# Decode attention on one Trainium2 core: the output weights loaded in eight parts that shrink, instead of three

## The chip, the cores and the metric

The kernel runs on one core of one Trainium2 chip (trn2). The metric is device time in microseconds (us) of one execution; smaller is better. Every run that is quoted was in the fast (undisturbed) state, and profiles are compared with profiles of that state. The profiled span, from the core's first to its last instruction, is some 1.9 us shorter than the device time.

## The reference, cut to what matters

One decode step for two sequences: attention with grouped heads over a long cache, an output projection, a gate from a small MLP, and a residual.

```python
B, Sq, D = 2, 1, 512
Hq, Hkv, Sk, Dh = 32, 8, 32768, 128          # all tensors bf16
...
q = (xn @ wq) ...
scores = einsum("bhqd,bhkd->bhqk", q, k) * Dh ** -0.5
o = einsum("bhqk,bhkd->bhqd", softmax(scores), v)
s = o.reshape(B, Sq, Hq * Dh) @ wo           # wo: 4096 x 512, 4 MB
return x + s * silu(mlp(xn))
```

K and V are 268 MB together. Each is read once, so the kernel is a long stream of loads with arithmetic running beside it. `wo` (4 MB) is the last thing that is loaded.

## The kernel before

The 16 pairs of sequence and K/V head are worked off one after the other. All large loads are issued from SyncE (SP) on one DMA queue, two large buffers being refilled in turn. The projection weights `wo` go into the part of `kbuf` that the last group no longer needs; they are issued behind the last V load, in three parts of four, three and one K/V heads:

```python
    wo_parts = [(0, 4), (4, 7), (7, 8)]
    ...
    for m in range(NG):                       # NG = 16 groups
        ...                                   # scores of one K half, next K load, the other half
        for i in range(NPART):
            emit_v(m, hs[i], i, eps[i])       # P times V; the last half also normalises into oX
        if not last:
            load_v(*groups[m + 1], 2 if m == NG - 2 else 1)
        if m == NG - 2:
            wo3 = kbuf[:, 0:Hq * D].rearrange("p (g c) -> p g c", g=Hkv)
            wos = A_wo.rearrange("(g p r) d -> p g (r d)", p=128, r=NQ)
            for a, z in wo_parts:
                nc.sync.dma_start(out=wo3[:, a:z, :], in_=wos[:, a:z, :])
```

The tail is 128 small matmuls, 16 for each K/V head, that accumulate into `s_ps`. Then come two VectorE steps (`sg`, the gate, and `out4`, the residual) and two stores of 1 KB each, one from SyncE and one from ScalarE:

```python
    for gr in range(Hkv * NQ):
        g, r = divmod(gr, NQ)
        for n in range(NQ):
            c = r * D + n * QW
            nc.tensor.matmul(s_ps[32 * n:32 * n + B, :], lhsT=oX[:, g, r, :],
                             rhs=wo3[:, g, c:c + QW], ...)
    ...
    for b, eng in ((0, nc.sync), (1, nc.scalar)):
        eng.dma_start(out=out[b, 0, :].rearrange("(n c) -> n c", c=QW), in_=out4[b:QP:32, :])
```

The framework gives every load and store that is issued from SyncE or ScalarE one of eight completion semaphores, in turn.

The softmax here doesn't subtract the row's maximum and nothing guards it: scores larger than these inputs give would overflow.

## Time and profile before

| | before |
|---|---|
| time, median of 3 runs | 660.86 us (660.72 to 660.88) |
| profiled span | 658.9 us |
| bytes moved, rate over the span | 280.9 MB, 426 GB/s |
| last packet of `wo` written | 653.68 us |
| `sg` starts | 654.71 us |
| SyncE issues its output store | 655.43 us |

The page of the kernel before comes first. Its DMA row gives the busy share of the 16 DMA engines in tenths for each of 40 slices; the queue rows give packets, megabytes and share of the engines' time; the last line gives shares of the chain that ended last.

```profile
span 658.9 us, 6323 instructions
...
DMA  9999999999999999999999999999999999999995
...
q1 hardware_dynamic: 6408, 280.50, 98.6%
q8 instruction: 21, 0.34, 0.2%
...
q14 instruction: 7, 0.06, 0.0%
...
DMA 75%; DVE 14%; issue 7%; PE 3%; SPq 0%; ACT 0%; DVEq 0%
```

The loads bound the kernel from start to end. What a change to `wo` can reach is the last slice. The timeline of that slice, before (start in us, duration, engine, line, operation, count; in brackets the engine's idle time before it and what ended it):

```profile
649.70 1.09 PE L400 MATMUL s_ps<-kbuf,oX 128*2 128x128 bf16 x64
652.79 1.88 PE L400 MATMUL s_ps<-kbuf,oX 128*2 128x128 bf16 x64 [2.00 <-DMA kbuf<-in_A_wo_dram]
654.71 0.29 DVE L408 TENSOR_TENSOR sg<-s_ps,g 98x128 f32<-98x128 f32 x1 [4.53 <-PE s_ps L400]
655.11 0.29 DVE L410 TENSOR_TENSOR out<-sg,x 98x128 bf16<-98x128 f32 x1
655.43 0.66 SPq L412 DMA_DIRECT2D out_dram<-out  x1
655.43 0.61 ACTq L412 DMA_DIRECT2D out_dram<-out  x1
```

PE does the first four heads at once, waits 2.00 us for the second part, and then has 64 matmuls to do in one piece.

The third view is busy time by stretch of the tail, before (stretch, its length, busy us and instructions of five engines, granted clock, DMA share, GB/s):

```profile
647.50:649.50 2.00, 1.08 (x12) 0.99 (x9) 0.16 (x1) 0.59 (x1) 0.00 (x0) 1.00 0.97 387
649.50:652.50 3.00, 1.26 (x68) 1.07 (x68) 0.34 (x2) 0.00 (x0) 0.00 (x0) 0.68 0.54 220
652.50:654.00 1.50, 1.21 (x48) 1.21 (x48) 0.00 (x0) 0.00 (x0) 0.00 (x0) 0.50 0.26 101
```

The DMA engines do not stop together. From 649.5 us on about half of them still work, and from 652.5 on five of 16 (the share of 0.26 takes in the last 0.3 us, when these too have ended). The landing records of the last part show it: seven engines report by 650.00 us, four by 652.44 and five by 653.99. Only the slowest ones decide when a part of `wo` has landed.

### The profile page before, as it was taken

What the parts mean: (1) busy time and instruction counts of PE and PEld (TensorE: products, weight loads), DVE (VectorE), ACT (ScalarE), POOL (GpSimd) and SP (SyncE); (2) the same over time, 40 slices, a digit from 0 to 9 for tenths busy, and PEclk for the clock granted to TensorE, in tenths of its full rate; (3) what the DMA queues carried; (4) which work ended last, traced back from release to release, by engine and by line L of the source; (5) the groups of instructions that cost most, each with busy time, mean ns of one, the idle gap of its engine ahead of it and who ended that gap; (6) DMA issues with size and microseconds to landing.
All of it is one profiled execution on the core that took longest, in us unless ns stands there. A gap on an engine that the chain in (4) does not pass through costs nothing.

```text
span 658.9 us, 6323 instructions
## 1 busy us (share of the span) xinstructions
PE 386.7 (59%) x2652; PEld 172.1 (26%) x2684; DVE 346.0 (53%) x442; ACT 50.3 (8%) x152; POOL 6.9 (1%) x20
## 2 busy tenths in 40 slices
PE   2338194673828557283764729377482946738764
PEld 2313132231313223131331313123131322313322
DVE  5147192754809265381935629183572918447560
ACT  1301001010100101000010100101010010100000
POOL 4000000000000000000000000000000000000000
PEclk9999688786968968697886959878596877859896
DMA  9999999999999999999999999999999999999995
GB/s 367 451 426 442 435 446 439 410 443 426 439 438 435 430 435 422 447 434 423 442 427 442 438 419 434 443 434 443 414 423 446 443 442 443 410 427 428 431 421 224
DMA packets 6704, 280.91 MB, mean 426 GB/s; under 512 B 906, under 2 KB 916, under 8 KB 1940
## 3 DMA queue, kind: packets, MB, share of 16 engines
q1 hardware_dynamic: 6408, 280.50, 98.6%
q8 instruction: 21, 0.34, 0.2%
q0 software_dynamic: 256, 0.01, 0.0%
q14 instruction: 7, 0.06, 0.0%
q10 hardware_dynamic: 12, 0.00, 0.0%
HBM read 280.50 MB, written 0.00 MB: 426 GB/s over the span
## 4 chain that ended last, share of the span: by engine, by line
DMA 75%; DVE 14%; issue 7%; PE 3%; SPq 0%; ACT 0%; DVEq 0%
DMA kbuf<-in_A_k_cache_dram 69%; DVE T L303 14%; DMA kbuf<-in_A_wo_dram 6%; PE sc L311 2%; PE o L343 1%; PE s_ps L400 0%; ACT ep L320 0%; SPq L95 0%; DVE pt L322 0%; SPq L115 0%; SPq L392 0%; SPq L114 0%; SPq L101 0%; PE S L339 0%; DVE sg L408 0%
## 5 line engine op out<-in xcount | busy, mean ns | idle before, releaser
L311 PE MATMUL sc<-T,z 128*128 128x512 bf16 x992 | 276.4, 421 | 206.3 <-DVE T L303 197.8
L303 DVE STREAM_TRANSPOSE T<-kbuf 128x1024 int32<-128x1024 int32 x256 | 291.5, 1205 | 150.5 <-DMA kbuf<-in_A_k_cache_dram 150.5
L311 PEld LDWEIGHTS <-z 128*128 128x128 bf16 x1024 | 105.7, 103 | 371.2 <-issue 278.7
L343 PE MATMUL o<-vbuf,pt 128*16 128x512 bf16 x1024 | 69.9, 434 | 3.2 <-DMA vbuf<-in_A_v_cache_dram 3.2
L320 ACT ACTIVATE ep<-sc 128x512 bf16<-128x512 f32 x32 | 19.1, 597 | 493.2 <-PE sc L311 451.2
L334 DVE MEMSET o<- 128x512 f32 x16 | 7.8, 485 | 69.3 <-ACT ob L352 68.3
L322 DVE STREAM_TRANSPOSE pt<-ep 128x512 bf16<-128x512 bf16 x32 | 22.6, 707 | 34.7 <-ACT ep L320 34.4
L343 PEld LDWEIGHTS <-pt 128*16 128x16 bf16 x1024 | 27.2, 99 | 37.9 <-issue 18.2
L339 PE MATMUL S<-sm,ones_f 128*128 128x4 f32 x64 | 10.7, 238 | 26.1 <-DVE sm L338 26.1
L355 PE MATMUL oT<-sel_o,ob 128*128 128x4 f32 x128 | 16.9, 255 | 11.1 <-ACT ob L352 11.1
L355 PEld LDWEIGHTS oT<-sel_o,ob 128*128 128x128 f32 x128 | 15.5, 191 | 19.3 <-ACT ob L352 19.3
L339 PEld LDWEIGHTS S<-sm,ones_f 128*128 128x128 f32 x64 | 10.7, 188 | 30.9 <-DVE sm L338 28.4
L352 ACT COPY ob<-o 128x512 f32<-128x512 f32 x16 | 9.4, 586 | 83.4 <-PE o L343 83.4
L362 DVE TENSOR_TENSOR on<-oT,rec 128x4 bf16<-128x4 f32 x16 | 2.6, 162 | 21.8 <-PE oT L355 21.8
L286 ACT COPY z<-qr 32x16 bf16<-32x16 bf16 x64 | 12.6, 198 | 11.5 <-DVE qr L233 10.9
L360 DVE RECIPROCAL rec<-S 128x4 f32<-128x4 f32 x16 | 2.9, 182 | 7.6 <-PE S L339 7.6
L365 PEld LDWEIGHTS <-sel_r 128*128 128x128 bf16 x64 | 5.2, 117 | 5.2 <-issue 5.2
L320 ACT ACTIVATION_READ_ACCUMULATOR ep<-sc 128x1 f32 x32 | 6.3, 198 | 0.2
L215 PE MATMUL qT_ps<-xT,kbuf 128*128 128x2 bf16 x128 | 3.6, 165 | 4.5 <-DMA kbuf<-in_A_wq_dram 4.5
L365 PE MATMUL xp<-on,sel_r 128*128 128x4 bf16 x64 | 3.8, 164 | 4.1 <-DVE on L362 4.1
L338 DVE TENSOR_SCALAR sm<-sel_h,rs 128x4 f32<-128x4 f32 x32 | 6.0, 188 | 0.0
L370 DVE TENSOR_TENSOR xm<-xp,mask 128x16 f32<-128x16 f32 x16 | 2.8, 174 | 5.3 <-PE xp L365 5.3
(64 smaller groups left out, 48.5 us busy)
## 6 DMA issues: line engine op xcount, KB each, us to landing
kbuf<-in_A_k_cache_dram SPq DMA_DIRECT2D x2, 4096.0 KB, 29.1
vbuf<-in_A_v_cache_dram SPq DMA_DIRECT2D x2, 4096.0 KB, 26.7
kbuf<-in_A_wq_dram SPq DMA_DIRECT2D x1, 4096.0 KB
vbuf<-in_B_w_dram SPq DMA_DIRECT2D x2, 1792.0 KB, 21.6
kbuf<-in_A_wo_dram SPq DMA_DIRECT2D x1, 2048.0 KB, 35.9
kbuf<-in_A_wo_dram SPq DMA_DIRECT2D x1, 1536.0 KB, 39.1
kbuf<-in_A_wo_dram SPq DMA_DIRECT2D x1, 512.0 KB
kbuf<-in_A_k_cache_dram SPq DMA_DIRECT2D x15, 29.4
```

Of the source, the lines that this page charges most:

```text
L286: nc.scalar.copy(out=z[32 * j:32 * j + 32, :, :, c:c + rep], in_=qr[32 * j:32 * j + 32, :, :, b, g * rep:(g + 1) * rep],)
L303: nc.vector.transpose(out=T[:, :].rearrange("p (b t k) -> p t b k", b=NB, t=RT), in_=kt[:, r * W:(r + 1) * W].rearrange("p (t b k) -> p t ...
L311: nc.tensor.matmul(sc[:, :], lhsT=z[:, nb, e, zc:zc + 128], rhs=Tb[:, nb, :, e], start=(r == 0 and nb == 0 and e == 0), stop=(r == NR - 1 ...
L320: nc.scalar.activation(out=ep[:, :], in_=sc[:, :], func=ACT.Exp, scale=inv_sqrt_dh, accum_out=rs[:, :])
L322: nc.vector.transpose(out=pt[:, :, :].rearrange("p r (t h) -> p t r h", h=rep), in_=ep[:, :].rearrange("p (t r h) -> p t r h", r=NR, h=rep),)
L334: nc.vector.memset(state["o"][:, :], 0.0)
L338: nc.vector.tensor_scalar_mul(out=sm[:, :], in0=sel_h[:, :], scalar1=rs[:, 0:1])
L339: nc.tensor.matmul(S[:, :], lhsT=ones_f[:, :], rhs=sm[:, :], start=(i == 0), stop=(i == NPART - 1))
L343: nc.tensor.matmul(o[32 * j:32 * j + VT * rep, :], lhsT=pt[:, r, a * VT * rep:(a + 1) * VT * rep], rhs=vt[:, u * VT:(u + 1) * VT, :].rearr ...
L352: nc.scalar.copy(out=ob[:, :], in_=o[:, :])
L355: nc.tensor.matmul(oT[:, :], lhsT=ob[:, t * Dh:(t + 1) * Dh], rhs=sel_o[:, t, :], start=(t == 0), stop=(t == VT - 1),)
L365: nc.tensor.matmul(xp[:, r, :], lhsT=sel_r[:, r, :, :].rearrange("p j w -> p (j w)"), rhs=on[:, :], start=True, stop=True,)
```

## The change

The intent is that PE should work off `wo` as it arrives, and that almost nothing should be left to do when the last bytes land. The last head is cut into 256, 128 and 128 KB.

```diff
-    wo_parts = [(0, 4), (4, 7), (7, 8)]
+    wo_parts = [
+        (0, 2, 0, 4), (2, 4, 0, 4), (4, 5, 0, 4), (5, 6, 0, 4),
+        (6, 7, 0, 4), (7, 8, 0, 2), (7, 8, 2, 3), (7, 8, 3, 4),
+    ]
...
-            for a, z in wo_parts:
-                nc.sync.dma_start(out=wo3[:, a:z, :], in_=wos[:, a:z, :])
+            for a, z, c, e in wo_parts:
+                nc.sync.dma_start(
+                    out=wo3[:, a:z, c * D:e * D], in_=wos[:, a:z, c * D:e * D]
+                )
```

## The prediction

> **What bounds the kernel now.** The load stream. The page gives 280.9 MB in 658.9 us, 426 GB/s, the DMA row of the 40 slices is almost all 9; the chain of waits is 75% DMA. So only the tail after the last byte can move. The timeline there: the second half of the last V releases PE at 644.15 us; the last attention group runs to 650.2; 64 projection matmuls (heads 0 to 3) start at 649.70; PE then idles 2.00 us for wo; at 652.79 the second part (three heads) lands and 64 matmuls run without a break for 1.88 us (29 ns each, granted clock 0.5); `sg` starts at 654.71, the output is issued at 655.43, the span ends at 658.9.
>
> The DMA packets in the trace add what the timeline hides. The 16 DMA engines are not in step: completions of one transfer come from seven engines first, five some 2.8 us later, four some 4.3 us later. In half-microsecond windows the DMA share falls from 1.0 to 0.6 at 649.5 and to 0.3 at 652.5. Every landing is that of the slowest four. They end the second wo part near 652.43, 0.36 us before PE starts on it, and the third near 653.68, which so reaches PE near 654.04. PE comes to that head (after 48 matmuls) near 654.2. Between that landing and `sg` lie about 0.65 us, all that finer parts can shorten.
>
> **What the change does.** Same 4 MB, order and queue.
> - Removes: the backlog. Heads 4, 5 and 6 land 1.25 us apart, near 650.3, 651.5 and 652.8, worked off as they come; after the last 128 KB four matmuls remain instead of a run of 64. PE tail after the last landing from 0.65 to about 0.2 us: -0.45 us.
> - Adds: shorter packets. A packet of 32 KB took 1,213 ns, one of 4 KB 159 ns, which gives about 8 ns per packet beside the bytes (estimate). Half of the last head then goes in 2 KB and half in 1 KB pieces: per engine 8 x 84 + 16 x 46 = 1.40 us against 1.27, +0.13 us. Five more completions: no cost shows in the spacing of the parts (1.248 us), so 0 to 0.1. The Trainium skill, "DMA: Bandwidth & Descriptors", section Bandwidth, gives 0.95 us for a 64 KB transfer and says to batch to 1 MiB or more, which should not apply to parts queued behind others.
> - Moves: in the built order 32 projection matmuls stand before the last group's last steps (21 before `oT`, 11 before `xp`). They need the first 1 MB, which should land near 646.7, before `o` ends at 647.5, and fit into PE's 0.7 us wait for the ScalarE copy. The last two wo transfers wait for the V halves' semaphores (eight are shared), at the latest near 644.7, with some 3 us of queue still ahead. No cost.
>
> **Sum.** -0.45 + 0.13 + about 0.05 = -0.3 us of 660.86, or 0.04%. Predicted 660.6 us, 659.9 to 661.2. Chances: faster by over 2% 0.005, within 2% 0.99, slower by over 2% 0.005.
>
> **What would show it.** `sg` starts 0.2 to 0.5 us earlier; the DMA still ends near 653.8; PE has several short waits for wo instead of one of 2.00 us; just four matmuls after the last; span 0.1 to 0.5 us shorter.
>
> **What would make it wrong.** 1 KB packets costing 100 ns or more; the late issue starving engines (DMA share falling before 649); the reordered matmuls delaying `oT` past 648.3; a different skew of the DMA engines.

## The result, and the profile after

| | before | after |
|---|---|---|
| time, median of 4 runs each | 660.79 us (660.57 to 660.88) | 659.69 us (659.62 to 659.87) |
| ratio of fast runs, 95% interval | | 0.9984 (0.9969 to 0.9998) |
| profiled span | 658.9 us | 658.0 us |

A ratio is the mean time of one kernel's fast runs over the mean of the other's fast runs of the same rounds, so it is not quite the ratio of the medians quoted here. The gain is 1.10 us where 0.3 had been forecast, and 659.69 lies below the predicted range.

The timeline of the tail, after (columns as before):

```profile
646.54 0.50 PE L405 MATMUL s_ps<-kbuf,oX 128*2 128x128 bf16 x21 [0.56 <-DMA kbuf<-in_A_wo_dram]
...
649.00 0.81 PE L405 MATMUL s_ps<-kbuf,oX 128*2 128x128 bf16 x32 [0.49 <-DMA kbuf<-in_A_wo_dram]
...
650.32 0.60 PE L405 MATMUL s_ps<-kbuf,oX 128*2 128x128 bf16 x16 [0.51 <-DMA kbuf<-in_A_wo_dram]
...
651.54 0.59 PE L405 MATMUL s_ps<-kbuf,oX 128*2 128x128 bf16 x16 [0.63 <-DMA kbuf<-in_A_wo_dram]
...
654.07 0.09 PEld L405 LDWEIGHTS <-oX 128*2 128x2 bf16 x3 [0.23 <-issue]
654.39 0.29 DVE L413 TENSOR_TENSOR sg<-s_ps,g 98x128 f32<-98x128 f32 x1 [5.46 <-PE s_ps L405]
...
655.11 0.65 SPq L417 DMA_DIRECT2D out_dram<-out  x1
```

Busy time by stretch, after (columns as before):

```profile
649.50:652.50 3.00, 1.50 (x44) 0.91 (x36) 0.00 (x0) 0.00 (x0) 0.00 (x0) 0.50 0.56 223
652.50:654.00 1.50, 1.20 (x28) 0.67 (x28) 0.00 (x0) 0.00 (x0) 0.00 (x0) 0.50 0.27 94
```

Up to `sg` everything is as forecast. The single wait of 2.00 us has become several short ones. Only the last four matmuls run after the last landing (the line at 654.07 has the weights of three of them; those of the first were loaded ahead). `sg` starts at 654.39 instead of 654.71, 0.32 us earlier. The stream ends at the same place: the last packet of `wo` is written at 653.74 instead of 653.68. The two halves of the DMA tail look the same.

The rest of the gain lies behind `sg`. From `sg` to the end of the span the kernel before took 658.94 - 654.71 = 4.22 us and the changed one 658.00 - 654.39 = 3.61 us, a difference of 0.61 us, although both execute the same two VectorE steps and the same two stores there. The trace has SyncE's closing list of waits. These are the starts of its entries in us, with the landings of the two stores between them (listed from the trace's records; S is a semaphore):

```
before   656.15 S110   656.23 S100   [landed: 657.10 S102, 657.27 S113]
         657.11 S102   657.29 S113   657.76 S114   657.85 S115   657.92 S116   657.99 S117   658.05 S118
after    655.82 S110   655.89 S100   655.96 S102   656.02 S113   656.08 S114   656.14 S115   656.20 S116
         [landed: 656.75 S118, 657.04 S117]   657.06 S117   657.12 S118
```

Each entry takes about 62 ns. Before, the stores had the semaphores that stand third and fourth in the list of nine entries (102, 113), so SyncE stopped there until the output had landed and still had five entries to go through. One of those steps, from 657.29 to 657.76, took 0.47 us instead of 0.06. After, five more transfers had moved the turn of the eight semaphores on by five. The stores now have the last two (117, 118), and the other entries are passed while the output is still in flight.

From the last landing to the end of the span: 658.94 - 657.27 = 1.66 us before, 658.00 - 657.04 = 0.96 us after. The flight of the stores (SyncE's issue to the last landing) was 1.84 us before and 1.94 us after. So the 0.93 us between the spans are 0.32 (up to `sg`), -0.09 (flight) and 0.70 (closing list). The remaining 0.17 us between the spans' difference and that of the medians is within the spread of the runs: the profiled run of the changed kernel was its slowest (659.87 us, 0.18 above the median).

### The profile page after: what moved, and what is told of

It reads as the page before. It is cut to its first block, busy times and chain, and to the rows that moved or that the text cites. A ratio compares the mean times of both kernels' runs of the same rounds, so it can differ in the third digit from the quotient of the medians.

```text
span 658.0 us, 6362 instructions
## 1 busy us (share of the span) xinstructions
PE 393.5 (60%) x2684; PEld 172.1 (26%) x2684; DVE 345.4 (52%) x442; ACT 50.2 (8%) x152; POOL 6.9 (1%) x20
## 4 chain that ended last, share of the span: by engine, by line
DMA 75%; DVE 15%; issue 7%; PE 2%; ACT 0%; SPq 0%; DVEq 0%
DMA kbuf<-in_A_k_cache_dram 69%; DVE T L303 14%; DMA kbuf<-in_A_wo_dram 5%; PE sc L311 1%; PE o L343 1%; PE s_ps L405 0%; PE oT L355 0%; DVE pt L322 0%; ACT ep L320 0%; ACT ob L352 0%; SPq L115 0%; SPq L114 0%; SPq L101 0%; PE S L339 0%; DVE sg L413 0%
## 5 line engine op out<-in xcount | busy, mean ns | idle before, releaser
L311 PE MATMUL sc<-T,z 128*128 128x512 bf16 x1024 | 281.7, 422 | 200.5 <-DVE T L303 194.7
L405 PE MATMUL s_ps<-kbuf,oX 128*2 128x128 bf16 x128 | 4.3, 266 | 2.9 <-DMA kbuf<-in_A_wo_dram 2.8
```

The costliest lines, as they stand in the source:

```text
L311: nc.tensor.matmul(sc[:, :], lhsT=z[:, nb, e, zc:zc + 128], rhs=Tb[:, nb, :, e], start=(r == 0 and nb == 0 and e == 0), stop=(r == NR - 1 ...
```

## The experiments

Theory 1: two thirds of the gain have nothing to do with the size of the parts. They come from which semaphores the output stores get, and from the one slow step in SyncE's closing list. Theory 2: all of the gain comes from the finer parts. The measure that tells them apart is the time from the last landing of an output store to the end of the span, together with the start of `sg`.

### First try: rotating the semaphores with spare loads, three kernels

Small loads that nothing reads were added on ScalarE's queue; the framework put them near the start. The order of the other instructions is unchanged, but with five and with three loads SyncE has one more wait near its start (90 records instead of 89, 97 instead of 96).

```diff
+    spare = pers.tile([B, 6 * 32], BF16)
...
+        if 1 <= m <= 5:                       # 3 or 1 in the other two
+            nc.scalar.dma_start(out=spare[:, 32 * m:32 * m + 32], in_=A_x[:, 0, 0:32])
```

The kernel before plus five:

> The kernel before, with five 64-byte-row loads that nothing reads added on ScalarE's queue near the start. They rotate the eight completion semaphores, so that the two output stores get the seventh and eighth, as in the changed kernel, instead of the second and third. Theory 1 (the end of the program waits for the eight in a fixed order, about 65 ns each, and one slow step of 0.4 us lies behind the third): 0.6 to 0.7 us faster than before, near 660.1 us; sg starts at the same distance from the last landing as before. Theory 2 (all of the gain comes from the finer parts of wo): the same as before within 0.15 us, or slower by what the five loads cost.

The changed kernel plus three:

> The changed kernel with three such loads, which rotate the output stores back to the second and third semaphore, as before. Theory 1: it keeps only the 0.3 us that the finer parts save up to sg, so 0.3 to 0.4 us faster than before and 0.6 to 0.7 us slower than the changed kernel. Theory 2: as the changed kernel, 1.1 us faster than before.

The changed kernel plus one:

> The changed kernel with one such load: one output store gets the eighth semaphore, the other the first. The closing list then stops at its first entry until the output has landed and has all other entries still to go through. Theory 1: at least as slow as the changed kernel with three such loads, 0.7 to 0.9 us slower than the changed kernel. Theory 2: as the changed kernel.

Measured: 661.80, 661.60 and 662.04 us, against 660.96 for the kernel before in the same rounds. All three are slower than before. Theory 1 had not expected that, and theory 2 only as a possible cost of the five loads. In their traces the last packet of `wo` is written at 655.18, 655.20 and 655.53 us instead of 653.7. The mean 64 KB packet took 2,424.5 ns in all three, against 2,421.2 before. The spare tile had been put in front of the two large buffers and had moved both by 384 bytes. As a test of the total time these three runs failed; whether the loads or the addresses did it was left to the next set. Their ends already fitted theory 1: 0.96, 1.21 and 1.47 us from the last landing to the end.

### Eight parts, but the last head whole

```diff
+    wo_parts = [(g, g + 1, 0, 4) for g in range(8)]     # in the changed kernel
```

> wo in eight parts of one head each (512 KB, 4 KB packets), the last not divided further; the semaphores fall as in the changed kernel. If the small last parts matter: 16 projection matmuls instead of 4 remain after the last landing (29 ns each, +0.35 us), but the last landing comes 0.13 us earlier, so 0.2 us slower than the changed kernel. If only the number of transfers matters (semaphores): the same as the changed kernel within 0.1 us.

Measured: 660.06 us against 660.96 (ratio 0.9986). The timeline of its tail:

```profile
654.11 0.60 PE L402 MATMUL s_ps<-kbuf,oX 128*2 128x128 bf16 x16 [0.63 <-DMA kbuf<-in_A_wo_dram]
654.11 0.30 PEld L402 LDWEIGHTS <-oX 128*2 128x2 bf16 x15 [0.82 <-issue]
654.75 0.29 DVE L410 TENSOR_TENSOR sg<-s_ps,g 98x128 f32<-98x128 f32 x1 [4.76 <-PE s_ps L402]
```

`sg` starts at 654.75, no earlier than the 654.71 of the kernel before: eight parts of one head each gain nothing there, because the last 16 matmuls wait for the last 512 KB just as in the kernel before. Still the kernel is 0.90 us faster, and its span is 0.74 us shorter, all of it behind `sg` (0.90 us from the last landing to the end instead of 1.66). So the finer cut of the last head alone is what brings `sg` forward. Cutting it into 2 KB and 1 KB packets made the last packet of `wo` no more than 0.02 us later (653.74 against 653.72), where 0.13 had been estimated.

### The rotation again, with the large buffers in place

The same added loads, but with the spare tile in a pool behind all others, so that the buffers keep their addresses.

```diff
+    spp = ctx.enter_context(tc.tile_pool(name="spp", bufs=1))   # after all other SBUF pools
+    spare = spp.tile([128, 6 * 32], BF16)
```

The kernel before plus five:

> As the first rotation run (before plus five small loads), but the spare tile lies behind all others, so that the big K and V buffers keep their addresses. Theory 1 (closing list): from sg to the end 3.5 to 3.7 us instead of 4.2, the stream ends near 653.7 again, total 660.1 to 660.3 us, 0.6 us faster than before. Theory 2 (all from finer parts): as before, within 0.15 us. Theory 3 (any small load slows the whole stream): 661.5 us and packets of 64 KB longer than 2,418 ns, as in the first run.

The changed kernel plus three:

> The changed kernel plus three such loads with the big buffers in place: output stores on the second and third semaphore. Theory 1: sg near 654.4, sg to the end 3.75 (if the slow step of the closing list stays hidden, as in the first run) to 4.2 us; total 659.9 to 660.4 us, slower than the changed kernel by 0.15 to 0.6. Theory 2: 659.7 us, as the changed kernel.

The changed kernel plus one:

> The changed kernel plus one such load with the big buffers in place: output stores on the eighth and first semaphore, so that eight entries of the closing list remain after the landing. Theory 1: sg to the end 4.0 us (as in the first run) against 3.6, total 660.1 us, 0.4 us slower than the changed kernel. Theory 2: 659.7 us.

Measured: 660.02 us (659.89 to 660.14), 660.04 us and 660.28 us, against 660.81 us (660.56 to 660.95) for the kernel before. The 95% intervals of the ratios are wide (0.9977 to 1.0002 for the first), but every run of the first is faster than every run of the kernel before, and the trace shows where the time went: its span is 0.60 us shorter, with 0.91 us from the last landing to the end instead of 1.66. The timeline of the kernel before plus five:

```profile
652.85 1.88 PE L404 MATMUL s_ps<-kbuf,oX 128*2 128x128 bf16 x64 [2.63 <-DMA kbuf<-in_A_wo_dram]
652.85 1.58 PEld L404 LDWEIGHTS <-oX 128*2 128x2 bf16 x63 [2.78 <-issue]
654.78 0.29 DVE L412 TENSOR_TENSOR sg<-s_ps,g 98x128 f32<-98x128 f32 x1 [6.01 <-PE s_ps L404]
```

Its tail up to `sg` is that of the kernel before, with the same run of 64 matmuls in 1.88 us and `sg` 0.07 us later. Yet it is 0.79 us faster in the median. Five loads that nobody reads bring most of the gain of the change; theory 2 falls. Undoing the rotation in the changed kernel (plus three) leaves `sg` at 654.45 and takes back some 0.3 us: it is 0.77 us faster than before where the changed kernel was 1.10. That is within what theory 1 expected: the slow step stays hidden, and from `sg` to the end it takes 3.92 us, between the 3.75 and 4.2 named. With one added load, where the list has the most entries left after the landing, some 0.6 us are taken back (0.53 us faster than before), a little more than the 0.4 expected.

### The addresses alone

```diff
+    shift = pers.tile([128, 6 * 32], BF16)        # 384 bytes in front of kbuf and vbuf, no load
+    nc.gpsimd.memset(shift[:, :], 0.0)
```

> The kernel before with 384 bytes of unused tile in front of the K and V buffers and no added load. If the shifted addresses slowed the first rotation runs: 1.2 to 1.5 us slower than before (stream end near 655.2, 64 KB packets 2,424.5 ns on average instead of 2,421). If the added loads did it: as before.

Measured: 662.42 us against 660.81, 1.6 us slower, with 64 KB packets of 2,424.6 ns on average and the last packet of `wo` at 655.73. (The profile is that of its slowest run, 663.05 us.) The addresses slowed the first set, not the loads. The buffers started at a multiple of 512 bytes before and 384 bytes past one here. Each engine takes some 240 of the 64 KB packets, so 3.4 ns more for each make 0.8 us, about half of the loss; where the rest arises, and what makes such a start slower, is not shown.

### Moving the slow step

In four traces so far (before, the two of five added loads, the shifted one) the slow step followed the 79th profiled instruction of SyncE, whichever semaphore stood there. Eight tiny copies on SyncE turn the semaphores around once, so that the stores keep their places in the list, but push that list eight instructions down.

```diff
+        if 1 <= m <= 8:
+            nc.sync.dma_start(out=spare[0:B, 4 * m:4 * m + 4],
+                              in_=oX[0:B, groups[m][1], :, groups[m][0]])
```

> The kernel before with eight tiny copies (8 bytes per row, on-chip) issued from SyncE, one each in eight of the middle groups. Eight transfers rotate the semaphores once around, so the output stores keep the second and third, as before; but SyncE's program becomes at least eight instructions longer ahead of the output store. If the slow step of 0.44 us stands at a fixed place of SyncE's program (after its 79th instruction, as in four traces so far), it falls among the wo loads, and sg to the end takes 3.9 us instead of 4.2: 0.2 to 0.4 us faster than before. If the slow step belongs to the closing list itself (its fourth or fifth entry), nothing changes, or the eight copies make it slower.

Measured: 660.35 us against 660.84, 0.49 us faster than before with eight transfers more. The 95% interval of the ratio, 0.9981 to 1.0006, takes in 1; of the five runs only the slowest (660.75) reaches into the range of the kernel before (660.72 to 661.03), and the trace shows the place. `sg` starts at 654.71 as before, and the last output landing is at 657.27 as before. From there to the end it takes 1.21 us instead of 1.66. A gap of 0.46 us still follows SyncE's 79th instruction, but that one is now the issue of the first part of `wo`, from 612.5 to 612.9 us, where nothing waits for it. The traces of the eight whole heads and of both changed kernels plus three have the gap at the same count (0.42, 0.44 and 0.42 us), among the issues of `wo`. In the changed kernel itself SyncE waits 2.65 us at that count, so there the step cannot be seen, only that it is gone from the end. The gain is a little more than expected (3.76 us from `sg` to the end instead of 3.9). What the step is, the traces do not say.

The traces fit one sum, but for the kernels plus one, with n the number of entries that follow, in the closing list, the entry of the store that landed last:

| kernel | n | slow step visible | last landing to end, us | 0.90 + 0.062 n, plus 0.44 |
|---|---|---|---|---|
| before plus five, buffers in place | 0 | no | 0.91 | 0.90 |
| eight whole heads | 0 | no | 0.90 | 0.90 |
| after | 1 | no | 0.96 | 0.96 |
| before plus eight on SyncE | 5 | no | 1.21 | 1.21 |
| after plus three, buffers in place | 6 | no | 1.27 | 1.27 |
| after plus one, buffers in place | 7 | no | 1.47 | 1.33 |
| before | 5 | yes | 1.66 | 1.65 |
| before, buffers shifted | 5 | yes | 1.66 | 1.65 |

The two constants are read from these rows, so the table shows that they are consistent, not where the 0.90 us comes from. The row that misses had 0.14 us more in the closing exchange between the engines, behind the list, and the first kernel plus one (1.47 us) had the same. In both, ScalarE has a slow step of its own just there: the gap after its 191st profiled instruction is 0.38 us, where the other kernels have 0.07 at this place of the exchange. In both kernels plus three the 191st instruction is the issue of the store, and the step follows it (0.34 us instead of 0.04), where it costs nothing.

### What puts the DMA engines out of step

The prediction took the staggered end of the DMA engines as given. In the trace the 21 packets of 16 KB on queue q8 fetch the instructions of PE. They come at intervals of 6 to 41 us and take 0.88 to 0.97 us each. The packet records do not name the engine, but packets of one engine follow one another without a gap. Strung together in this way, as far as the strings can be told apart, the fetches fall on eight engines in turn.

A fetch costs its engine more than its own time: the kernel before has 22 packets of 64 KB that took over 2.6 us instead of 2.418, and each of them begins within 16 ns of the end of a fetch. Together, fetch and longer packet delay the engine by 1.43 us for 16 KB on q8, and by 0.84 to 0.85 us for five of the six 8 KB fetches on queue q14 in the stream. Two and three times 1.43 us are 2.9 and 4.3 us, the two lags that the prediction had read from the landings.

To test whether the fetches make the stagger, every second P times V matmul was left out, which gives a wrong result and leaves all loads of data as they are:

```diff
-        for u in range(KPT // VT):
+        for u in range(0, KPT // VT, 2):              # in the changed kernel
```

> The changed kernel with every second matmul of the P times V product left out, so PE's program is 1,024 rows shorter; the result is wrong on purpose, all loads stay. It tests what puts the 16 DMA engines out of step. If it is the fetching of PE's program (16 KB at a time, 0.93 us each, on eight engines in turn): 17 fetches instead of 21, hardly any engine serves three before the end, so the group of four that ends last (4.3 us behind the first) shrinks to one or none, and in the half-microsecond windows the DMA share after 652.5 is near 0.06 to 0.1 instead of 0.3; the last landing comes 0 to 1.5 us earlier, depending on one engine that serves other fetches. If the lag has another cause (the engines themselves, HBM): groups of seven, five and four as before, and the last landing at 653.7.

Measured: 659.61 us against 660.84 (the changed kernel had 659.69 in its own rounds). With 512 matmuls and 512 weight loads fewer there are 17 fetches, 16 of them before 650 us (two for each of the eight engines), where the changed kernel has 20. Busy time by stretch:

```profile
649.50:652.50 3.00, 1.36 (x65) 0.92 (x65) 0.35 (x2) 0.00 (x0) 0.00 (x0) 1.00 0.55 211
652.50:654.00 1.50, 1.01 (x32) 0.56 (x31) 0.00 (x0) 0.00 (x0) 0.00 (x0) 0.94 0.05 16
```

After 652.5 us the DMA share is 0.05 instead of the 0.27 of the changed kernel: one engine of 16 instead of five. The landings of the last part now come from seven engines by 650.10 us, eight by 652.63 and one at 653.86. That is what the theory of instruction fetches had said. The last packet of `wo` comes only 0.20 us earlier (653.54), because one engine still lags. In the strung packets that engine is the one with gaps of 0.3 us at the times of five of the 8 KB fetches of queue q14. Five times 0.84 us are 4.2 us, which is its lag. This last assignment is read from the records; no run tested it.

## Why the prediction was right or wrong

- "So only the tail after the last byte can move": right. The last packet of `wo` moved by 0.06 us.
- "PE tail after the last landing from 0.65 to about 0.2 us: -0.45 us" and "+0.13 us" for the shorter packets: right in sum, in part by luck. With the same 0.36 us of delivery, from the last packet to `sg` remained 0.67 us before and 0.29 after, so -0.38; the landing came 0.06 us later. Together -0.32 us, where -0.3 was forecast: both terms were 0.07 us too large, and the errors cancel. The eight-whole-heads run shows that the gain comes from the small last parts.
- "Moves: ... No cost": right. `oT` was done before 648.1 us, `o` before 646.1, and the last issues of `wo` starved no engine (DMA share 0.99 until 649.5).
- "Every landing is that of the slowest four": right for the first part of `wo` in the kernel before, which seven, five and four engines ended in turn. For its last two parts the groups are seven, four and five; between them comes PE's fetch at 647.8 us, which fits one more engine set back. The shortened PE program showed what sets all but one of them back.
- The step that failed is "Sum. -0.45 + 0.13 + about 0.05 = -0.3 us". The sum stops at `sg` and takes the 4.2 us behind it as fixed. The prediction even named the eight shared semaphores, but asked only whether the loads wait for them. In place of that zero the runs measured an end, from the last landing on, that is 0.70 us shorter (0.61 us from `sg` to the end, the flight of the stores being 0.09 us longer). Five more transfers moved the stores from the third and fourth entry of the list to the last two (0.062 us for each entry, four entries fewer behind the last landing: 0.25 us), and the slow step of 0.44 us is no longer behind it. The kernel before with nothing but five dummy loads was 0.79 us faster. The range, 659.9 to 661.2 us, was too narrow because the end was not among the terms.

The gains do not add up across the experiments, and should not: rotation and the moved step each remove the same visible 0.44 us. Both kernels that are faster than before without finer parts (plus five, plus eight) stay behind the changed kernel, and no run found a correct kernel that beats it.

## What to carry to other kernels

Price the program's end as carefully as the loop: after the last computation there were still 3.5 us, and the part of them behind the last landing ran from 0.90 to 1.66 us with the places of the stores and of the slow step. When a change adds or removes transfers, look where the output stores come to stand in the closing waits before crediting the gain to the change itself. A control run that adds only harmless transfers costs little and tells the two apart, provided that it moves no buffer.

## What the Trainium skill lacked or had wrong

- "Runtime: NRT & Kernel Launch", section "The ~15µs preamble/postamble breakdown", lists the closing barrier and the resets with one time for each, and no list of waits before them. The runs show a part that depends on the kernel: SyncE walks a list of waits at about 62 ns an entry, and the last landing to the end took 0.90 to 1.66 us, with the places of the output stores in it and with the slow step of the next point.
- No page has the step of 0.42 to 0.46 us that follows SyncE's 79th profiled instruction: 0.44 before, 0.45 with five added loads, 0.43 with shifted buffers, 0.46 with eight added copies (at 612.9 us), 0.42 with eight whole heads. ScalarE shows one after its 191st (0.34 and 0.38 us with three and one added loads).
- "Runtime: NRT & Kernel Launch", section "Instruction fetch mechanics", calls the cost of crossing a fetch boundary mostly hidden and gives blocks of 16 KiB. PE's fetches here are 16 KB (21 packets, 0.34 MB), others 8 KB. Each of PE's sets one DMA engine back by 1.43 us (0.93 us of its own, and 0.5 by which the next packet is longer), and in a kernel bound by loads that matters: the last engines ended some 4.3 us behind the first. With 17 fetches instead of 21, the DMA share at the very end fell from 0.27 to 0.05.
- "DMA: Bandwidth & Descriptors", section "Rules for kernel authors", asks for 1 MiB or more per DMA. It does not separate a transfer that stands alone from one with a backlog before it. Here parts of 128 KB behind others made the last landing 0.06 us later, with packets of 4, 2 and 1 KB taking 159, 84 and 46 ns.
- The same page, section "How a descriptor splits into AXI transactions", speaks of descriptors that do not start at a multiple of 256 bytes, without a cost for a shifted destination in SBUF. Buffers 384 bytes past a multiple of 512 made 64 KB packets 3.4 ns longer on average and the kernel 1.6 us slower.
